# Reordering the first loads and the start-up steps of a packed-attention and gated-FFN kernel

## The chip, the cores and the metric

The kernel runs on one core of one Trainium2 chip. The metric is device time in microseconds (us) of one execution, the median of several runs; lower is better. Engines are named as the profile names them: PE (TensorE matmul), PEld (its weight loads), DVE (VectorE), ACT (ScalarE), POOL (GpSimd) and SP (SyncE, which here only issues DMAs; SPq in the rows).

## What is computed

For 8 batches and 8 heads, 32 packed queries `p` first attend to 576 keys and values, and the 576 queries `q` then attend to the 32 packed results. The heads are joined to a 512-wide row for each of 8 x 576 = 4608 tokens, and a gated feed-forward layer follows.

```python
def sm_attn(qq, kk, vv):
    s = scale * np.matmul(qq, kk.transpose(0, 1, 3, 2))
    s = s - np.max(s, axis=-1, keepdims=True)
    a = np.exp(s)
    a = a / (np.sum(a, axis=-1, keepdims=True) + 1e-09)
    return np.matmul(a, vv)
p_packed = sm_attn(p, k, v)                  # softmax 1: 32 x 576 per head
out = sm_attn(q, p_packed, p_packed)         # softmax 2: 576 x 32 per head
x = out.transpose(0, 2, 1, 3).reshape(B * S, H * D)
return (x @ w_a) * (x @ w_b) @ w_out         # 512 -> 1536 (twice) -> 512
```

## The kernel before

**The algebra.** The attention output is never formed. For each batch and slice of weight columns the kernel multiplies the packed results with the weights first (`g_tiles`, L357, 16 matmuls at L371, "G"), and then G with the softmax-2 weights (`mm1`, L394, matmuls at L389). The product of the two halves is h; `mm2_part` (L412) multiplies it with w_out. Large products run as three passes on a high and a low word (hi x hi, hi x lo, lo x hi). The high word is a cast on ACT, the low word a subtraction on DVE or POOL (`lo_part`, L90).

**Order of work.** `manual_schedule` (L570) keeps every engine, SP too, in the order in which the program emits its instructions. So the order is written by hand, as strings of short names that `emit` (L458) reads:

- `FIRST` (L499): the first loads on SP. `k0`, `k1` are heads 0 to 3 and 4 to 7 of batch 0's k for its first 512 tokens (512 KB each, `load_first`, L131), `k2` the last 64 tokens of all heads (128 KB); the same for q. `p0` is three DMAs of 32 KB (`load_p`), `v0` and `v1` are one of 512 KB and two of 32 KB each (`load_v`), `w1` is one raw weight piece of 512 KB (`load_w`).
- `START` (L500): what follows before the first `mm1`. `T0` turns p and `P0` the packed results (two PE transposes, one copy, L241 and L243). `k0`..`k4` and `q0`..`q4` turn the loaded k and q on PE (`turn_first`, L142): n = 0, 1 use part 0, n = 2, 3 part 1, n = 4 part 2; the copy out of PSUM is on DVE or ACT, as `TURN` (L503) says for each. `S0` starts softmax 1 of the even heads (e = 0); every `r0` is its next step (score matmuls L255; maximum and exponential; reciprocal; transposes L291; product with v L301); `r1` and `S1` step the odd heads (e = 1). `s0` and `s1` step softmax 2 of the two halves (`stage2`, L310): score matmuls L316; transpose and maximum on DVE (L321, L325); subtraction (L328); exponential on ACT (L330); sum and reciprocal on DVE, scaling (L334 to L337); transpose into `a2f` on DVE (L341) and high-word cast on ACT (L347); low word on DVE. `SUBS` (L504) says for each batch and half whether the subtraction and the scaling are on DVE ("1") or POOL ("0").
- `A`, `B`, `C`: the weights arrive as 36 raw pieces (24 of w_a and w_b, numbered 0 to 23, then 12 of w_out) and each goes through three conversions, in order of the pieces: A is the high word on ACT (L194), B the low word (L196) on ACT, DVE or POOL as the piece's digit in `WAYS` (L502) says ("0", "1", "2"; L202 for ACT, L199 for the other two), C joins them on DVE (L205) and frees the raw buffer, upon which SP loads a further piece. There are 12 raw buffers. `D` splits a finished w_out piece (cast on ACT, low word on POOL). G of a pair of slices needs four C more than the pair before.
- `W` (L557): nine matmuls on data already there, whose result nobody uses; they fill PE. `g` is the first G. `Lk`, `Lq`, `Lv`, `Lp` are loads for batch 1 and later.
- `PLAN_0` (L509): the same names for batch 0's 12 slices of `mm1` (24 slots, two for each slice: one between its two halves, one at its end) and the first of `mm2` after it; `PLAN` (L506) for batch 1. `k0` and `k1` of batch 1 are DVE transposes (L124), its `S0` stands in slot 11.

**Buffers that tie the engines together.** `mm1` takes two PSUM bank pairs "m" in turn. ACT empties one (`asb`, L401), DVE multiplies the other with it (L404), ACT casts the product (L408) and POOL makes its low word (`h_lo`, L91). `asb` has two buffers, so that slice n+2 needs the `h_lo` of slice n. G, the turned tiles and several transposes share two PSUM banks "x". At most eight DMAs of SP are under way: the ninth waits for the first to land, and so on.

After batch 1 the kernel goes over to another scheme (L685 on) for batches 2 to 7, which the change does not touch.

Of the kernel before, what the change touches and what calls it, by code (L numbers as in the profile page):

```python
# [19 lines left out]
def tile_packed_attn_gated_ffn(  # L20
# [21 lines left out]
    B, H, S, D = q.shape  # L42
# [50 lines left out]
    def bank():  # L93
        return ps_x.tile([P, 512], F32, name="x")

    def bank_pair(s=False):
        return ps_s.tile([P, 2, 512], F32, name="s") if s else ps_m.tile([P, 2, 512], F32, name="m")
# [44 lines left out]
    def turn_first(key, n):  # L142

        if (0, key) not in xTs:
            pool = scratch if key == "q" else ld
            xTs[0, key] = [pool.tile([P, R, HS], F32, name=f"xT{i}") for i in range(2)]
        copy = (nc.vector.tensor_copy, nc.scalar.copy)[int(TURN["kq".index(key) * 5 + n])]
        x = bank_pair()[:, 0, :] if n in (2, 3) else bank()
# [47 lines left out]
    def low_word(raw, way):  # L196
        low = raw[..., 0]
        if way:
            (nc.vector if way == 1 else nc.gpsimd).tensor_scalar(  # L199
                out=low, in0=low, scalar1=2.0 ** -29, scalar2=7.0, op0=ALU.mult, op1=ALU.min)  # L200
        else:
            nc.scalar.activation(out=low, in_=low, func=AF.Copy, scale=0.93 * 2.0 ** -29)  # L202
# [107 lines left out]
    def stage2(b, e):  # L310
# [15 lines left out]
        yield  # L326
        eng = nc.vector if b < 2 and SUBS[2 * b + e] == "1" else nc.gpsimd
        eng.tensor_tensor(out=s2, in0=s2, in1=mx.unsqueeze(2).broadcast_to([P, TU, J]), op=ALU.subtract)  # L328
# [125 lines left out]
    def drain(g):  # L454
        for _ in g:
            pass

    def emit(b, plan, tasks={}):  # L458

        for name in plan.split():  # L460
            if name in tasks:
                next(tasks[name], None)
                continue
            if name == "W":
                warm()
                continue
            if name in "ABCD":
                convert(name)
                continue
            what, e = name[:-1], int(name[-1])  # L470
            n = b + (e // 2 if b or what[0] == "L" else 0)
            if n >= B:
                continue
            if what == "S":
                if e == 0:
                    st[b] = [stage1(b, 0), stage1(b, 1), stage2(b, 0), stage2(b, 1)]
                next(st[b][e])
            elif what == "s":
                next(st[b][2 + e], None)
            elif what == "r":  # L480
                next(st[b][e], None)
            elif what == "T":
                turned(pT, p_nat.pop(n))
            elif what == "P":
                turned(ppT[:, b % 2:b % 2 + 2], pp.pop(b), b % 2)
            elif what in ("k", "q"):
                turn(what, n, e % 2) if b else turn_first(what, e)
            elif what == "Lk":
                load(k, "k", n, e % 2)
            elif what == "Lq":  # L490
                load(q, "q", n, e % 2)
            elif what == "Lv":
                load_v(n, e % 2)
            elif what == "Lp":
                load_p(n)

    st = {}

    FIRST = ("p0 k0 k2 k1 q0 v0 q1 v1 q2 w1 w1 w1 w1 w1 w1 w1 w1 w1 w1 w1")  # L499
    START = ("T0 k0 k4 k1 k3 k2 q0 S0 S1 r0 r1 q1 r1 r0 r0 r1 r0 q2 r1 q3 q4 P0 s0 B s1 W A s0 B A A s0 s0 B s1 C "  # L500
             "A s1 B s0 C s1 A s1 C B B Lp2 C A B A s0 s1 B C B B s0 B g A C A A s1 Lv2 Lk2 C C A A C B B Lk3 C s1")
    WAYS = ("000000022220202120012012011200010010")  # L502
    TURN = ("0001110101")  # L503
    SUBS = ("0100")  # L504

    PLAN = (" |  |  | S0 | r0 | r0 |  | r0 |  | r0 Lv1 ; S1 | r1 | r1 q0 Lk2 | r1 | r1 | q1 Lk3 Lv2 P0 |  ; s0 | s0 s0 | s0 T2 | "  # L506
            "s0 Lp4 | s0 s1 | s1 s1 | s1 | s1 | s1 | t0 t1 t2 t3 u0 | k2 |  | k3 Lq2")
    PLAN = dict(enumerate(PLAN.split("|")))
    PLAN_0 = ("A | C C | B A B A | B C C B C | A A | C | B | C B A T0 k0 Lp2 A | A A B B C Lq0 | C C k1 | A B A | "  # L509
# [3 lines left out]
    PLAN_0 = dict(enumerate(PLAN_0.split("|")))  # L513

    pieces = [(c, n) for c in range(NC) for n in range(4)] + [(NC, f) for f in range(NFT)]
# [12 lines left out]
    def convert(x):  # L528
# [14 lines left out]
        elif x == "B":  # L543
            low_word(raw, int(WAYS[pieces.index((c, n))]))
        else:
# [18 lines left out]
    def next_g(b):  # L564

        g_tiles(b, *(((0, 1), (2,)) if b else ((0, 1),)), s=True)
        yield

    ET = mybir.EngineType
    ep(tc.manual_schedule(engines={ET.PE, ET.DVE, ET.Activation, ET.Pool, ET.SP}))  # L570
    for name in FIRST.split():
        what, i = name[0], int(name[1])
# [8 lines left out]
    tasks = {"g": next_g(0)}  # L581
    emit(0, START, tasks)
    drain(tasks["g"])
# [53 lines left out]
    for b in range(NB):  # L637
        plan = dict(PLAN if b else PLAN_0)
        slot, tasks, late_steps = [0], {"g": next_g(b + 1)} if b == 0 else {}, [""]
# [316 lines left out]
```

## Time and profile before

| | |
|---|---|
| median of 3 runs | 715.3 us (714.02, 715.3, 716.52) |
| the profiled execution | 714.0 us, of which the span of its instructions is 712.2 us |
| START (to the first `mm1` matmul) | 34.7 us |
| batch 0 (`mm1`, `mm2`) up to the first `mm1` of batch 1 | 34.7 to 122.9 us |
| the untouched scheme of batches 2 to 7 | from about 172 us on |

A row of a timeline reads: start, duration, engine, line, operation, what it writes and reads, shapes, count, and in brackets the time for which the engine had been idle before and what released it. A row of a table by stages reads: the stretch, its length, then for each engine its busy time and its number of instructions, the granted TensorE clock, the mean busy share of the DMA engines and their rate in GB/s.

### The profile page before, as it was taken

To read this page: it belongs to the slowest core of one execution; us is meant where nothing else is said; L and a number is where in the kernel's file an instruction comes from. 1 tells how busy PE (TensorE), PEld (TensorE's weight loads), DVE (VectorE), ACT (ScalarE), POOL (GpSimd) and SP (SyncE) were. 2 spreads that over 40 slices of the span, in tenths; PEclk is the share of its full clock that TensorE was granted. 3 is DMA by queue.
4 is the path that set the end of the run, shared out by engine and by line. 5 is a ranking of instruction groups with operands and counts; after the bars stand their busy time and mean duration, and the time that the engine had idled before them with its cause. 6 is when DMAs were issued, how large, how long until landed. Compare 5 with 4: busy or idle time off the path is not lost.

```text
span 712.2 us, 14198 instructions
## 1 busy us (share of the span) xinstructions
PE 699.0 (98%) x5558; PEld 574.2 (81%) x5558; DVE 449.8 (63%) x819; ACT 363.2 (51%) x733; POOL 417.8 (59%) x322
## 2 busy tenths in 40 slices
PE   6899999999999999999999999999999999999998
PEld 4488877888778887887888788788888888888887
DVE  3888755367455669665875668765785657754342
ACT  3788753554344455644563456554554455544520
POOL 0496753337334687745874579566776578856520
PEclk9999999999999999999999999999999999999999
DMA  8999872767344735555453574457146323133002
GB/s 230 387 274 315 220 162 53 193 153 282 93 98 139 211 96 141 139 138 146 134 111 115 142 195 93 106 176 182 61 98 180 105 89 119 61 110 127 1 1 74
DMA packets 177059, 102.37 MB, mean 144 GB/s; under 512 B 141280, under 2 KB 159456, under 8 KB 171616
## 3 DMA queue, kind: packets, MB, share of 16 engines
q1 hardware_dynamic: 176992, 101.47, 50.3%
q8 instruction: 43, 0.70, 0.4%
q14 instruction: 24, 0.20, 0.1%
HBM read 85.72 MB, written 15.73 MB: 142 GB/s over the span
## 4 chain that ended last, share of the span: by engine, by line
PE 94%; DVE 2%; SPq 1%; DMA 1%; ACT 1%; issue 0%; DVEq 0%; ACTq 0%
PE x L724 37%; PE m L765 29%; PE m L389 9%; PE x L779 5%; PE m L415 5%; PE s L301 2%; PE s L316 1%; PE s L255 1%; PE x L371 1%; PE s L291 1%; SPq L116 1%; DMA kn<-in_k_dram 1%; DMA nat<-in_k_dram 0%; PE m L152 0%; PE x L152 0%
## 5 line engine op out<-in xcount | busy, mean ns | idle before, releaser
L724 PE MATMUL x<-wo,h_hi 128*128 128x512 f32 (+1 forms) x776 | 249.3, 391 | 0.0
L91 POOL TENSOR_TENSOR h_lo<-asb,h_hi 128x576 fp32r<-128x576 f32 x96 | 140.3, 1462 | 83.3 <-ACT h_hi L810 44.6
L724 PEld LDWEIGHTS x<-wo,h_hi 128*128 128x128 f32 x776 | 140.8, 188 | 22.2 <-ACT gs L785 1.0
L724 PE MATMUL x<-wo,h_lo 128*128 128x512 f32 (+1 forms) x388 | 152.1, 392 | 0.0
L91 POOL TENSOR_TENSOR G_lo<-gs,G_hi 128x640 fp32r<-128x640 f32 x72 | 113.0, 1575 | 30.6 <-ACT G_hi L800 30.3
L724 PEld LDWEIGHTS x<-wo,h_lo 128*128 128x128 f32 x388 | 72.9, 188 | 11.8
L91 POOL TENSOR_TENSOR A_lo<-gs,A_hi 128x256 fp32r<-128x256 f32 x36 | 27.2, 754 | 89.7 <-ACT A_hi L788 89.7
L847 DVE TENSOR_TENSOR d<-m,d 128x576 f32<-128x576 f32 (+1 forms) x73 | 54.0, 740 | 34.6 <-ACT d L843 33.8
L860 DVE TENSOR_TENSOR asb<-m,d 128x288 f32<-128x288 f32 x72 | 32.4, 451 | 66.4 <-ACT c L856 64.8
L856 ACT COPY c<-m 128x288 f32<-128x288 f32 x72 | 28.8, 399 | 78.6 <-PE m L765 78.6
L734 DVE TENSOR_TENSOR part<-x,part 128x512 f32<-128x512 f32 (+1 forms) x65 | 44.1, 678 | 38.8 <-PE x L724 38.8
L765 PE MATMUL m<-tx_hi,G_hi 128*128 128x288 f32 x216 | 63.8, 296 | 0.0
L765 PE MATMUL m<-tx_hi,G_lo 128*128 128x288 f32 x216 | 63.7, 295 | 0.0
L785 ACT COPY gs<-x 128x512 f32<-128x512 f32 x36 | 21.1, 587 | 82.8 <-PE x L779 81.2
L765 PE MATMUL m<-tx_lo,G_hi 128*128 128x288 f32 x216 | 63.3, 293 | 0.0
L800 ACT CAST G_hi<-gs 128x640 fp32r<-128x640 f32 x72 | 52.2, 730 | 15.1 <-POOL gs L794 14.5
L843 ACT COPY d<-m 128x576 f32<-128x576 f32 (+1 forms) x73 | 46.6, 639 | 20.2 <-PE m L765 18.6
L810 ACT CAST h_hi<-asb 128x576 fp32r<-128x576 f32 x72 | 49.0, 680 | 11.5 <-DVE asb L874 11.5
L765 PEld LDWEIGHTS m<-a_hi,G_hi 128*128 128x128 f32 x144 | 27.0, 187 | 31.6 <-issue 17.4
L794 POOL TENSOR_TENSOR gs<-gs 128x512 f32<-128x512 f32 x36 | 46.7, 1296 | 2.6 <-DVE gs L791 2.5
L765 PE MATMUL m<-a_hi,G_hi 128*128 128x288 f32 x144 | 47.0, 326 | 0.0
L389 PE MATMUL m<-a_hi,ghi 128*128 128x288 f32 x192 | 43.2, 307 | 1.5 <-ACT ghi L377 1.5
(171 smaller groups left out, 1548.7 us busy)
## 6 DMA issues: line engine op xcount, KB each, us to landing
wr<-w_kept SPq DMA_DIRECT2D x36, 1024.0 KB
nat<-in_k_dram SPq DMA_DIRECT2D x56, 144.0 KB
nat<-in_q_dram SPq DMA_DIRECT2D x56, 144.0 KB
vt<-in_v_dram SPq DMA_DIRECT2D x28, 256.0 KB
out_dram<-part SPq DMA_DIRECT2D x27, 256.0 KB
raw<-in_moe_w_a_dram SPq DMA_DIRECT2D x12, 512.0 KB
raw<-in_moe_w_b_dram SPq DMA_DIRECT2D x12, 512.0 KB
raw<-in_moe_w_out_dram SPq DMA_DIRECT2D x12, 512.0 KB
```

Source lines behind the costliest of these rows:

```text
L91: return eng.tensor_tensor(out=dst, in0=src, in1=hi.bitcast(F32), op=ALU.subtract)
L389: nc.tensor.matmul(out=ps[:, half, 0:HS], lhsT=gt[:, kt, ft % 4, cols], rhs=at[:, kt, HS * half:HS * half + HS], start=(n == 0 and kt == 0 ...
L415: nc.tensor.matmul(out=o[:, cols], lhsT=ht[:, c0:c0 + P], rhs=wt[:, cols], start=(ft == 0 and n == 0), stop=(ft == NFT - 1 and n == 2))
L724: nc.tensor.matmul(out=o[:, cols], lhsT=ht[:, c0:c0 + P], rhs=wt[:, cols], start=(ft == fts[0] and n == 0), stop=end)
L734: nc.vector.tensor_tensor(out=parts[i][:, cols], in0=o[:, cols], in1=parts[i][:, cols], op=ALU.add)
L765: nc.tensor.matmul(out=bank[:, n % 2, 0:HS], lhsT=g, rhs=t, start=(first and i == 0), stop=(i == 2), skip_group_check=True)
L779: nc.tensor.matmul(out=gps[e][J * r:J * r + J, :], lhsT=ppT[rows, 2 * (b % 2), r, :], rhs=w[rows, r, :], start=True, stop=True)
L794: nc.gpsimd.tensor_tensor(out=gs[:, 2:4].rearrange("p a u f -> p a (u f)"), in0=gs[:, 0:2].rearrange("p a u f -> p a (u f)"), in1=s2.unsqu ...
L800: nc.scalar.copy(out=G_hi[:, n % 3], in_=gs[:, 1:6, n % 2])
L810: nc.scalar.copy(out=view(h_hi[ft]), in_=src)
L843: nc.scalar.copy(out=d[:, both], in_=X[:, both, 0:HS])
L847: nc.vector.tensor_tensor(out=d[:, both], in0=V[:, both, 0:HS], in1=d[:, both], op=ALU.add)
```

## The change

Only the strings change; `PLAN` is only joined into one literal. In `FIRST`, k2 and k0 go ahead of p0, q1 and q0 ahead of v0, and q2 goes behind three weight pieces. In `START`, `T0` moves behind k1, the turns of q and the steps of softmax 1 are interleaved otherwise, and the conversions stand at other places. `WAYS` gives 16 low words to POOL instead of 10, 9 to DVE instead of 7, 11 to ACT instead of 19; among the first 13, which are converted in START, POOL had 7, 8, 9, 10, 12 and now has 1, 5, 7, 9, 10, 11, 12. `TURN` swaps the engines of several copies. `SUBS` puts the subtraction and scaling of batch 0's second half on POOL; both were on DVE. In START `Lk2 Lk3` (k of batch 1) now stand ahead of `Lv2`. `PLAN_0` is written anew; the turns, softmax steps and loads of batch 1 keep nearly the same slots, and the conversions are spread otherwise.

```diff
-    FIRST = ("p0 k0 k2 k1 q0 v0 q1 v1 q2 w1 w1 w1 w1 w1 w1 w1 w1 w1 w1 w1")
-    START = ("T0 k0 k4 k1 k3 k2 q0 S0 S1 r0 r1 q1 r1 r0 r0 r1 r0 q2 r1 q3 q4 P0 s0 B s1 W A s0 B A A s0 s0 B s1 C "
-             "A s1 B s0 C s1 A s1 C B B Lp2 C A B A s0 s1 B C B B s0 B g A C A A s1 Lv2 Lk2 C C A A C B B Lk3 C s1")
-    WAYS = ("000000022220202120012012011200010010")
-    TURN = ("0001110101")
-    SUBS = ("0100")
+    FIRST = ("k2 k0 p0 k1 q1 q0 v0 v1 w1 w1 w1 q2 w1 w1 w1 w1 w1 w1 w1 w1")
+    START = ("k0 k4 k1 T0 k2 k3 S0 r0 q2 r1 q3 q0 S1 r0 r1 r0 r1 q1 r0 B r1 A A B q4 P0 s0 s0 s1 C s0 A s1 s1 W s0 B Lp2 C s0 B B s1 C A B B A A s1 A C A s0 B C A B B B s1 s0 s1 C B g A C A C A s1 C Lk2 Lk3 C Lv2 B")
+    WAYS = ("020002020222202022121112211201120120")
+    TURN = ("0110110010")
+    SUBS = ("0000")
...
-    PLAN_0 = ("A | C C | B A B A | B C C B C | A A | C | B | C B A T0 k0 Lp2 A | A A B B C Lq0 | C C k1 | A B A | "
-              "S0 B | B A r0 | C C C | B A Lq1 |  | C C B r0 r0 D A A | S1 C D | B C B B A D | r1 C | A A D | r0 T2 "
-              "|  | q0 B r1 C B D r1 C |  | A | D B C Lv1 A r1 | A B D Lk2 B C B q1 D Lk3 A A P0 | C s0 s0 D C Lp4 "
-              "A B | s1 s0 | Lv2 | D | s0 s1 s0 | k2 s0 s1 C k3 | s1 |  | Lq2 D s0 s1 s1 Lq3 s1")
+    PLAN_0 = ("A C | | A A | C | B C B B | A C B C C B B A | | A A T0 Lq0 B k0 A C | B Lp2 C A | B k1 C B | A C | C A S0 B | B r0 C A | Lq1 B C | A | C | r0 C r0 D B A | S1 A C B D | C A B D B | r1 C | r1 D | A r0 A C | T2 | B q0 D A r1 | | C B Lv1 A B D | C A r1 | A B Lk2 C B q1 D C P0 | D D s0 B Lk3 C | s0 Lv2 B s1 | s0 A Lq2 D s0 s1 | | | s0 k2 D s0 s1 s0 s1 C Lp4 s1 A k3 | | | s1 Lq3 s1")
```

More of the change, by code (lines that the diff above doesn't have):

```diff
@@ L497, in tile_packed_attn_gated_ffn @@
     st = {}
-    FIRST = ("p0 k0 k2 k1 q0 v0 q1 v1 q2 w1 w1 w1 w1 w1 w1 w1 w1 w1 w1 w1")
-    START = ("T0 k0 k4 k1 k3 k2 q0 S0 S1 r0 r1 q1 r1 r0 r0 r1 r0 q2 r1 q3 q4 P0 s0 B s1 W A s0 B A A s0 s0 B s1 C "
-             "A s1 B s0 C s1 A s1 C B B Lp2 C A B A s0 s1 B C B B s0 B g A C A A s1 Lv2 Lk2 C C A A C B B Lk3 C s1")
-    WAYS = ("000000022220202120012012011200010010")
-    TURN = ("0001110101")
-    SUBS = ("0100")
-    PLAN = (" |  |  | S0 | r0 | r0 |  | r0 |  | r0 Lv1 ; S1 | r1 | r1 q0 Lk2 | r1 | r1 | q1 Lk3 Lv2 P0 |  ; s0 | s0 s0 | s0 T2 | "
-            "s0 Lp4 | s0 s1 | s1 s1 | s1 | s1 | s1 | t0 t1 t2 t3 u0 | k2 |  | k3 Lq2")
+    FIRST = ("k2 k0 p0 k1 q1 q0 v0 v1 w1 w1 w1 q2 w1 w1 w1 w1 w1 w1 w1 w1")
[3 more added lines that the diff above has]
+    SUBS = ("0000")
+    PLAN = (" |  |  | S0 | r0 | r0 |  | r0 |  | r0 Lv1 ; S1 | r1 | r1 q0 Lk2 | r1 | r1 | q1 Lk3 Lv2 P0 |  ; s0 | s0 s0 | s0 T2 | s0 Lp4 | s0 s1 | s1 s1 | s1 | s1 | s1 | t0 t1 t2 t3 u0 | k2 |  | k3 Lq2")
     PLAN = dict(enumerate(PLAN.split("|")))
-    PLAN_0 = ("A | C C | B A B A | B C C B C | A A | C | B | C B A T0 k0 Lp2 A | A A B B C Lq0 | C C k1 | A B A | "
[3 rows of a table removed]
+    PLAN_0 = ("A C | | A A | C | B C B B | A C B C C B A | | A A T0 Lq0 B k0 A C | B Lp2 C A | B k1 C B | A C | C A S0 B | B r0 C A | Lq1 B C | A | C | r0 C r0 D B A | S1 A C B D | C A B D B | r1 C | r1 D | A r0 A C | T2 | B q0 D A r1 | | C B Lv1 A B D | C A r1 | A B Lk2 C B q1 D C P0 | D D s0 B Lk3 C | s0 Lv2 B s1 | s0 A Lq2 D s0 s1 | | | s0 k2 D s0 s1 s0 s1 C Lp4 s1 A k3 | | | s1 Lq3 s1")
     PLAN_0 = dict(enumerate(PLAN_0.split("|")))
```

## The prediction

> **What bounds the kernel now.** I read the page first, then a table by stages.
>
> ```profile
> span 712.2 us, 14198 instructions
> PE 699.0 (98%) x5558; PEld 574.2 (81%) x5558; DVE 449.8 (63%) x819; ACT 363.2 (51%) x733; POOL 417.8 (59%) x322
> ```
> ```profile
> 5.00:10.00 5.00, 3.00 (x17) 2.52 (x17) 1.12 (x2) 0.43 (x2) 0.00 (x0) 1.00 1.11 311
> 15.00:20.00 5.00, 4.46 (x100) 3.27 (x100) 2.23 (x11) 3.25 (x9) 0.00 (x0) 1.00 1.11 307
> 0.00:37.27 37.27, 27.61 (x270) 16.84 (x270) 21.90 (x43) 20.70 (x40) 10.67 (x12) 1.00 0.96 310
> 37.27:172.00 134.73, 134.49 (x1249) 113.57 (x1250) 88.94 (x142) 81.53 (x149) 73.39 (x49) 1.00 0.77 206
> 700.00:712.20 12.20, 9.17 (x52) 7.89 (x50) 2.92 (x5) 0.00 (x0) 0.00 (x0) 0.98 0.34 108
> ```
> PE is idle for 13.2 us in all: 9.66 before 37.27, 3.03 in the tail that the change leaves alone, and 0.24 in the rest of the stretch that `PLAN_0` governs and the start of the next. So the change can win only before 37.27, but can lose anywhere up to 172. Next, PE's timeline in the start.
>
> ```profile
> 7.08 1.12 PE L152 MATMUL x<-ident,kn 128*128 128x128 f32 x4 [2.00 <-DMA kn<-in_k_dram]
> ...
> 10.03 1.92 PE L152 MATMUL m<-ident,kn 128*128 128x128 f32 x8
> ...
> 17.89 0.66 PE L152 MATMUL m<-ident,qn 128*128 128x128 f32 x4
> ...
> 21.55 0.72 PE L316 MATMUL s<-xT,ppT 64*32 64x288 f32 x16 [0.61 <-DVE ppT L243]
> ...
> 23.46 7.99 PE L562 MATMUL m<-kn,ident 128*128 128x512 f32 x18
> 31.63 1.57 PE L371 MATMUL x<-w_ab,ppT 64*32 64x512 f32 x16 [0.17 <-DVE w_ab L205]
> 34.68 0.54 PE L389 MATMUL m<-a_hi,ghi 128*128 128x288 f32 x2 [1.48 <-ACT ghi L377]
> ...
> 37.27 0.54 PE L389 MATMUL m<-a_lo,ghi 128*128 128x288 f32 x2 [0.26 <-DVE a_lo L91]
> ```
> 7.99 us of PE's busy time are the filler `W`. The time is therefore set by when softmax 2 can start (21.55) and by how long DVE, ACT and POOL need from there to feed `mm1` without a break (37.27).
>
> **The start, up to s0.** SP's timeline and the chain of waits:
>
> ```profile
> 0.74 1.96 SPq L182 DMA_DIRECT2D p_nat<-in_p_dram  x3
> 2.74 0.48 SPq L135 DMA_DIRECT2D kn<-in_k_dram  x1
> ...
> 38.01 1.78 SPq L170 DMA_DIRECT2D vt<-in_v_dram  x2
> ```
> ```profile
> 2.74 4.30 DMA kn<-in_k_dram
> ...
> 39.99 6.69 PE m L389 x48
> ...
> 55.20 2.89 DMA nat<-in_k_dram
> ```
> With k2 alone ahead of it, k0 is issued at 0.74 plus one first issue, about 1.5, not 2.74. At 4.30 us to landing that is 5.8, not 7.04; the three small transfers of p no longer go ahead, which may spare up to 0.9. I take 5.5 (4.9 to 5.8). From k0's landing to the copy that ends `P0` took 13.9 us (7.04 to 20.98, below). Three things are added. `T0`, formerly done while PE waited for k0, now stands behind k1: 0.9. The copy of q4 moves from ACT to DVE, ahead of that of `P0`: 0.43 (row below). And turns of q now stand between the two halves of softmax 1, so that ACT makes two copies of q ahead of the second exponential: walked step by step, 0.3 net. So 5.5 + 15.5 = 21.0, and s0 at 21.5: no gain, although k lands 1.5 us earlier.
>
> The eight turns of k2 and k3 took 1.92 us at 10.03 and would take 1.3 at the later pace of 0.66 for four; the granted clock stands at 1.00 in both stretches. I count half of that difference as won, since PE now starts 1.5 us earlier and has no break. The Trainium skill ("TensorE: Matmul & The Clock Gate", Part 1) lets PE run fast after some 3.4 us of steady work; the trace still shows slow turns three us after 7.08. By the rule the sum would be 0.3 lower.
>
> q4 needs q2, which now goes behind three weight pieces: 5088 KB in all with k, p, q and v, 5.2 MB. At the 0.307 to 0.311 MB/us of the rows, from a start near 3.5, it lands at about 20.2. PE has done the turn's predecessors at 19.9, so q2 costs 0 to 0.3. The end of a transfer can trail the mean rate: k0's 512 KB at that rate are 1.7 us, not 4.30. So up to 1.2 more is the upper end.
>
> **From s0 to a steady `mm1`.**
>
> ```profile
> 20.61 0.43 ACT L159 COPY xT<-x 128x128 f32<-128x128 f32 x2 [1.44 <-PE x L157]
> ```
> ```profile
> 20.98 0.42 DVE L243 COPY ppT<-x 128x256 f32<-128x256 f32 x1 [0.29 <-PE x L241]
> 22.36 0.78 DVE L321 STREAM_TRANSPOSE s<-s 128x576 f32<-128x576 f32 x1 [0.96 <-PE s L316]
> ...
> 25.33 0.71 DVE L205 SCALAR_TENSOR_TENSOR w_ab<-raw 128x512 uint32<-128x512 uint32 x1
> ...
> 29.81 1.08 DVE L337 TENSOR_TENSOR s<-s,sum 128x576 f32<-128x576 f32 x1
> ...
> 32.01 1.42 DVE L341 STREAM_TRANSPOSE a2f<-s 128x576 f32<-128x576 f32 x2
> ...
> 34.66 1.29 DVE L91 TENSOR_TENSOR glo<-x,ghi 128x512 fp32r<-128x512 f32 x2
> ...
> 36.46 0.76 DVE L91 TENSOR_TENSOR a_lo<-a2f,a_hi 128x576 fp32r<-128x576 f32 x1
> ```
> ```profile
> 24.02 1.16 POOL L328 TENSOR_TENSOR s<-s,mx 128x576 f32<-128x576 f32 x1 [22.71 <-DVE mx L325]
> 28.03 1.41 POOL L337 TENSOR_TENSOR s<-s,sum 128x576 f32<-128x576 f32 x1 [2.86 <-DVE sum L336]
> 29.63 12.54 POOL L199 TENSOR_SCALAR raw<-raw 128x512 uint32<-128x512 uint32 x5 [0.19 <-DMA raw<-in_moe_w_b_dram]
> 42.24 1.43 POOL L91 TENSOR_TENSOR h_lo<-asb,h_hi 128x576 fp32r<-128x576 f32 x1
> ```
> ```profile
> L199 POOL TENSOR_SCALAR raw<-raw x10: 2000/2344/2971, 29.6 to 76.5; 128x512 uint32<-128x512 uint32 x10
> ```
> Now the walk for the second half, s1. Its transpose and maximum stand behind the first join C (0.71) and end at 26.05, where the old order had them at 25.4. The subtraction is on POOL (1.16): 27.3. The exponential on ACT stands behind two low words: 28.0. Sum and reciprocal on DVE, behind another C: 30.0. The scaling goes to POOL, too, and there B5 is emitted ahead of it. POOL scales the first half until 29.5, then B5 takes 2.0 to 2.5 (I take 2.3): 31.9. Then the scaling, 1.3: 33.3. Before, DVE had it at 30.9. So the transpose of s1 ends at 34.05, not 33.43. Behind it DVE has, in emitted order, two low words of a2f, one C and only then the low words of G (0.7, 0.7, 0.65, 0.65): the first at 36.75. The old order had G's low words ahead, at 34.66, and the second a2f word last. PE starts `mm1` near 34.9 but after four matmuls needs that word; where the old order had done 14 matmuls by 37.27, ten are left. At 6.69/48 = 0.139 each they end at 38.1. **Cost 0.85**, less 0.05 for s0. `W` and the first G change nothing: the filler runs until about 31.4 either way, and the fourth C is done by then.
>
> **POOL's backlog, 38 to 66 us.** The steps that follow on ACT:
>
> ```profile
> L377 ACT CAST ghi<-x 128x512 fp32r<-128x512 f32 x9 | 4.8, 583 | 0.0
> L408 ACT CAST h_hi<-asb 128x576 fp32r<-128x576 f32 x7 | 4.7, 671 | 2.7 <-DVE asb L404 2.7
> L401 ACT COPY asb<-m 128x576 f32<-128x576 f32 x7 | 4.5, 637 | 0.4 <-PE m L389 0.4
> ```
> ```profile
> 59.72 0.71 PE L255 MATMUL s<-xT,pT 64*32 64x288 f32 x20 [0.20 <-DVE xT L124]
> ```
> From 33.3 POOL has B7, B9, B10, B11, B12, two `h_lo`, B14. With B at 2.0 to 2.5, taken as 2.3 and then 2.1 once DVE joins less: B10 ends at 40.4, `h_lo` of slice 0 at 46.3 (43.7 before), B14 at 50.0. Who waits?
> - C10 (slot 0) waits on DVE for B10, with the product of slice 0 queued behind it: product at 41.8, cast 0.67, two casts of G 1.17, copy 0.64 on ACT: bank pair free at 44.25, PE wants it at 43.95. **0.3.**
> - C14 (slot 5) waits for B14; behind it stand C15, B18 and the low words of the third G until 52.4, which hold the "x" bank that `T0` of batch 1 needs; PE wants it at 51.8. **0.6.**
> - In slots 8 to 10 DVE has B20 to B22, k1, C and two low words of G ahead of the product of slice 5: 63.1, wanted at 62.65. **0.45.**
> - A gain: SP issues k of batch 1 ahead of v, so at least 1.78 earlier, and its last part, which landed at 58.09 (55.20 + 2.89), no longer holds up `S0` in the row of 59.72. The first four of its 24 matmuls were issued 0.88 ahead of the rest, of which they need 0.3. **-0.6.**
>
> At no B above 2.0 the first two items vanish; at 2.5 throughout they are 0.8 and 2.2.
>
> After 66 I count nothing. PE needs G and the w_out pieces far apart there, DVE, ACT and POOL are busy for 89, 82 and 73 of 135 us, and six more low words on POOL are 14 us in its gaps. Were the gaps not where the words fall, each could cost up to 2.3.
>
> **Sum.** 0.8 + 0.3 + 0.6 + 0.45 - 0.6 = 1.55: the profiled execution's 714.0 becomes 715.5. The median of the runs shown is 715.3, so I forecast 716.8. That is no change that a measurement of this kernel can tell, which takes about 0.3%, 2.15 us.
>
> **Rivals.**
> - *POOL's backlog in full* (slower). If B runs at the 12.54/5 = 2.5 of its busiest row, as it did with DVE joining beside it, the two stalls grow by 0.5 and 1.6: 718.9. It decides from 2.3 on. For it: seven of the first 13 low words are on POOL now and h_lo stands behind them. Against: DVE has idle time beside B5. 0.20.
> - *q2 late* (slower). All that follows shifts by up to 1.3: 718.1. For it: the three pieces ahead. Against: the mean rate holds it at 20.2. 0.12.
> - *An exclusive port* (slower). In the first 12.6 us of POOL's low words, DVE ran these joins beside them:
>
> ```profile
> 29.60:42.20 12.60, 7.07 (x10) 1.00 1.04 362
> ```
> Were they to add their full time to five words of 2.0, these would take 17.1, not 12.54. If now some nine two-input steps of 0.7 added theirs, B14 would end at 54.5 and the sum grow by 4.5: 721. The Trainium skill ("SBUF - State Buffer", SBUF: two separate sides) says that a GpSimd instruction and a DVE one with two SBUF inputs shut each other out for a whole instruction; by that rule this rival holds, by the trace a third of it does. 0.03.
> - *The early k comes through* (faster). k0 at 4.9 shifts all by -0.6, B at 2.0 brings the scaling 0.3 forward and takes the two stalls away: 716.8 - 0.6 - 0.3 - 0.9 = 715.0, and without the third 714.5. For it: 1.2 us fewer of issues ahead of k. Against: q2 and the longer chain behind k0. 0.23.
>
> **The numbers.** The forecast has 0.42. Slower by over 0.3%: the first three rivals, 0.35. Faster by over 0.3%: the last rival reaches that only with the 1.3 by which runs of one kernel differ (714.02 to 715.3), 0.14 with what I may have overlooked; the rest, 0.51, is no change. The range goes from 714.5 less 1.3, 713.2, to 718.9 with part of q2's delay, 719.6.
>
> **What would show it.** Right: k0's first turn near 5.6; s0 within 0.5 of 21.55; L337 twice on POOL, the second past 31.5 with an L199 between; the first `glo` behind both `a_lo`, near 36; PE idle near 44 and 52 for `asb` and `glo`; no idle time at batch 1's `S0`. Wrong: s0 at 20.5 or before, or past 22.5; `mm1` steady by 37; PE unbroken from there to 66; or new idle time of PE past 66.

## The result, and the profile after

| | before | after |
|---|---|---|
| median | 715.8 us (714.02 to 716.52) | 725.0 us (724.24 to 725.49) |
| profiled execution | 714.0, span 712.2 | 725.38, span 723.5 |

The ratio after to before is 1.0132 (95% interval 1.0110 to 1.0154): 9.3 us slower by the medians. The forecast was 716.8 with a range to 719.6. First the page of the kernel after:

```profile
span 723.5 us, 14200 instructions
...
PE 703.5 (97%) x5558; PEld 575.7 (80%) x5558; DVE 454.6 (63%) x820; ACT 358.4 (50%) x724; POOL 433.6 (60%) x330
```

Now its table by stages, cut where the steady `mm1` starts (40.37 instead of 37.27) and 11.2 us behind the place of before (172.00):

```profile
0.00:40.37 40.37, 28.13 (x261) 15.96 (x261) 20.40 (x41) 20.61 (x39) 14.43 (x14) 0.91 0.96 309
40.37:183.20 142.83, 138.33 (x1259) 116.05 (x1260) 95.17 (x145) 76.58 (x141) 85.11 (x55) 0.99 0.70 188
```

PE is idle for 12.24 us ahead of 40.37 (9.66 before) and for 4.50 in the second stretch (0.24 before). Over the whole execution it is also busy for 4.5 us more (703.5 against 699.0) with the same 5558 matmuls: some of them ran slower. PE's timeline in the start shows where:

```profile
22.39 0.77 PE L157 MATMUL x<-ident,qn 32*128 32x32 f32 x8 [2.28 <-DMA qn<-in_q_dram]
...
24.29 1.21 PE L316 MATMUL s<-xT,ppT 64*32 64x288 f32 x16 [0.52 <-DVE ppT L243]
...
26.40 9.55 PE L557 MATMUL m<-kn,ident 128*128 128x512 f32 x18
...
38.40 0.54 PE L389 MATMUL m<-a_hi,ghi 128*128 128x288 f32 x2 [1.43 <-ACT ghi L377]
...
40.37 0.85 PE L389 MATMUL m<-a_hi,glo 128*128 128x288 f32 x2 [1.17 <-DVE glo L91]
41.01 0.68 PE L389 MATMUL m<-a_hi,ghi 128*128 128x288 f32 x2
```

Three rows answer to rows of before. PE waits 2.28 us for q2, and s0 is at 24.29 instead of 21.55. The filler `W` takes 9.55 us instead of 7.99. The first `mm1` pairs from 41.01 on take 0.68 instead of 0.43. The granted clock of the TensorE (the third column from the right) says why:

```profile
20.00:25.00 5.00, 2.21 (x34) 1.41 (x34) 1.20 (x4) 1.28 (x2) 1.98 (x1) 0.77 1.06 357
25.00:30.00 5.00, 5.00 (x33) 1.92 (x14) 4.32 (x7) 1.17 (x3) 2.19 (x2) 0.54 1.05 384
...
40.00:45.00 5.00, 4.63 (x36) 4.14 (x36) 4.99 (x8) 1.69 (x3) 4.76 (x4) 0.68 0.83 258
```

It was 1.00 in these stretches before. Now POOL's and DVE's timelines in the start:

```profile
32.85 2.02 POOL L199 TENSOR_SCALAR raw<-raw 128x512 uint32<-128x512 uint32 x1
34.95 1.39 POOL L337 TENSOR_TENSOR s<-s,sum 128x576 f32<-128x576 f32 x1
36.42 10.57 POOL L199 TENSOR_SCALAR raw<-raw 128x512 uint32<-128x512 uint32 x5
```
```profile
36.37 0.78 DVE L341 STREAM_TRANSPOSE a2f<-s 128x576 f32<-128x576 f32 x1 [1.05 <-POOL s L337]
37.08 1.57 DVE L91 TENSOR_TENSOR a_lo<-a2f,a_hi 128x576 fp32r<-128x576 f32 x2
38.56 1.15 DVE L205 SCALAR_TENSOR_TENSOR w_ab<-raw 128x512 uint32<-128x512 uint32 x1
39.64 1.28 DVE L91 TENSOR_TENSOR glo<-x,ghi 128x512 fp32r<-128x512 f32 x2
```

As forecast, the second scaling (L337) stands behind a low word on POOL, and the first `glo` behind both `a_lo` and a join. Last, PE's waits behind 50, and the rows of DVE and of POOL that belong to the first two:

```profile
57.67 0.44 PE L241 MATMUL x<-ident,p_nat 128*128 128x128 f32 x2 [1.08 <-DVE glo L91]
...
64.80 0.53 PE L389 MATMUL m<-a_hi,ghi 128*128 128x288 f32 x2 [0.68 <-DVE asb L404]
...
66.59 0.72 PE L255 MATMUL s<-xT,pT 64*32 64x288 f32 x24
...
70.37 0.53 PE L389 MATMUL m<-a_hi,ghi 128*128 128x288 f32 x2 [0.74 <-DVE asb L404]
...
92.38 0.53 PE L389 MATMUL m<-a_hi,ghi 128*128 128x288 f32 x2 [0.62 <-DVE asb L404]
...
96.39 0.73 PE L415 MATMUL m<-wo,h_hi 128*128 128x512 f32 x2 [0.68 <-DVE asb L404]
```
```profile
54.48 2.54 DVE L205 SCALAR_TENSOR_TENSOR w_ab<-raw 128x512 uint32<-128x512 uint32 x2 [0.84 <-POOL raw L199]
56.94 1.28 DVE L91 TENSOR_TENSOR glo<-x,ghi 128x512 fp32r<-128x512 f32 x2
...
61.09 2.98 DVE L205 SCALAR_TENSOR_TENSOR w_ab<-raw 128x512 uint32<-128x512 uint32 x2
64.00 0.74 DVE L404 TENSOR_TENSOR asb<-m,asb 128x576 f32<-128x576 f32 x1
```
```profile
54.52 1.94 POOL L91 TENSOR_TENSOR h_lo<-asb,h_hi 128x576 fp32r<-128x576 f32 x1
...
61.04 1.43 POOL L91 TENSOR_TENSOR h_lo<-asb,h_hi 128x576 fp32r<-128x576 f32 x1
```

From 54.48 two joins take 2.54 us together, from 61.09 two take 2.98, where a pair in the flow takes 1.3. In each pair one join alone takes 1.93 (55.09 to 57.02 and 61.09 to 63.02), and beside each POOL runs an `h_lo`, until 56.46 and 62.47: both joins end 0.55 us behind it. The `glo` that frees `T0`'s bank and the product that PE awaits at 64.80 stand behind these joins.

**Where the 11.3 us of the two spans lie.** Three marks divide them: s0, the second G (38.80 before, 44.49 after) and the end. Up to s0 2.7 were lost, from s0 to the second G 2.95 (17.25 became 20.20), behind it 5.6 (673.4 became 679.0). I use the last two lengths for all runs below, since the start of s0 itself varies: in four runs with the same loads and the same steps up to it, e10, e11, e13 and e14, it was at 22.6 or 22.7 (22.0 in e5), where the profiled execution of before had 21.55. Part of the 2.7 is thus chance, and it fits that the medians differ by 9.3 and not by 11.3.

### The profile page after: what moved, and what is told of

The parts are those of the page before. It is cut to its first block, busy times and chain, and to the rows that moved or that the text cites. A ratio compares the mean times of both kernels' runs of the same rounds, so it can differ in the third digit from the quotient of the medians.

```text
span 723.5 us, 14200 instructions
## 1 busy us (share of the span) xinstructions
PE 703.5 (97%) x5558; PEld 575.7 (80%) x5558; DVE 454.6 (63%) x820; ACT 358.4 (50%) x724; POOL 433.6 (60%) x330
## 4 chain that ended last, share of the span: by engine, by line
PE 86%; DMA 4%; POOL 3%; DVE 3%; issue 1%; SPq 1%; ACT 1%; DVEq 0%; ACTq 0%; POOLq 0%
PE x L719 37%; PE m L760 29%; PE m L389 6%; PE x L774 5%; PE m L415 4%; PE s L301 1%; DMA raw<-in_moe_w_b_dram 1%; PE s L316 1%; DMA raw<-in_moe_w_a_dram 1%; POOL raw L199 1%; PE s L255 1%; DMA qn<-in_q_dram 1%; POOL h_lo L91 1%; DVE w_ab L205 1%; POOL wo L91 1%
## 5 line engine op out<-in xcount | busy, mean ns | idle before, releaser
L91 POOL TENSOR_TENSOR h_lo<-asb,h_hi 128x576 fp32r<-128x576 f32 x96 | 141.1, 1471 | 86.0 <-ACT h_hi L805 44.4
L91 POOL TENSOR_TENSOR G_lo<-gs,G_hi 128x640 fp32r<-128x640 f32 x72 | 113.1, 1576 | 30.6 <-ACT G_hi L795 30.3
L91 POOL TENSOR_TENSOR A_lo<-gs,A_hi 128x256 fp32r<-128x256 f32 x36 | 27.2, 755 | 89.6 <-ACT A_hi L783 89.6
L838 ACT COPY d<-m 128x576 f32<-128x576 f32 (+1 forms) x73 | 46.7, 640 | 20.1 <-PE m L760 18.5
L805 ACT CAST h_hi<-asb 128x576 fp32r<-128x576 f32 x72 | 49.0, 680 | 11.3 <-DVE asb L869 11.3
L389 PE MATMUL m<-a_hi,ghi 128*128 128x288 f32 x192 | 44.0, 311 | 3.5 <-DVE asb L404 2.0
```

Source lines behind the costliest of these rows:

```text
L91: return eng.tensor_tensor(out=dst, in0=src, in1=hi.bitcast(F32), op=ALU.subtract)
L389: nc.tensor.matmul(out=ps[:, half, 0:HS], lhsT=gt[:, kt, ft % 4, cols], rhs=at[:, kt, HS * half:HS * half + HS], start=(n == 0 and kt == 0 ...
L805: nc.scalar.copy(out=view(h_hi[ft]), in_=src)
L838: nc.scalar.copy(out=d[:, both], in_=X[:, both, 0:HS])
```

## The experiments

"Before" is the old kernel's median beside the run named. The theories were formed in turn; their numbers in the expectations are those of that time.

### The loads

e1 is the changed kernel with q2 ahead of all weight pieces, e2 the changed kernel with the whole old `FIRST`, e3 the old kernel with the changed `FIRST`.

```diff
-    FIRST = ("k2 k0 p0 k1 q1 q0 v0 v1 w1 w1 w1 q2 w1 w1 ...
+    FIRST = ("k2 k0 p0 k1 q1 q0 v0 v1 q2 w1 w1 w1 w1 w1 ...      # e1
```

> The changed kernel, with q2 loaded ahead of the weight pieces again and nothing else altered. Changed kernel: 725.0 us, softmax 2 (s0) at 24.3, filler from 26.4 to 35.9, first mm1 matmul at 38.4. Theory A (q2's place costs a wait of 2.3 us and, through the cold clock, 0.5 more, and everything behind moves with it): s0 at 21.7, first mm1 near 35.4, 721.8. Theory B (the filler, stretched by the cold clock, gates the first G as well): 720.3. Theory C (the steps on DVE and POOL after 40 us set the end whatever happens before): above 723.5.

> The changed kernel with the whole old order of the first loads (p0 k0 k2 k1 q0 v0 q1 v1 q2 w...). k0 then lands at 7.04 instead of 5.1, q2 at 17.6 instead of 22.2. If the long chain behind k0 (15 us from k0 to the turn of q4) sets s0, s0 comes at about 23.5 and the time is 724; if the place of q2 is all that the load order cost, s0 comes at 21.6 and the time is 721.8.

> The kernel before with only the new order of the first loads. Theory A: q4 has to wait for q2 as in the changed kernel (landing at 22.2 instead of 17.6), s0 at about 24, a cold clock, and +2.7 to +3.2 us: 718.5 to 719. If the load order costs nothing by itself in the old order of steps: 715.8.

Measured, beside 715.1 for before: e1 722.84 (ratio 1.0115, 1.0095 to 1.0136), e2 725.41 (1.0152, 1.0132 to 1.0171), e3 715.88 (1.0014, 1.0002 to 1.0026). By e1, q2's late landing costs the changed kernel some 2.2 us if the two medians are compared, 1.5 if each is taken against the before beside it. This size is not settled: in e2 q2 is early, too, and s0 came at 22.5 instead of 24.3, but nothing was gained. In the old order of steps the new loads cost 0.8. Most of the loss lies in the steps.

### The clock

e4 is the changed kernel with three filler matmuls ahead of the turn of q4; e9 is e1 with three between the first G and the first `mm1`.

```diff
-  ... A A B q4 P0 ...            # e4, from the changed START
+  ... A A B V q4 P0 ...
-  ... C B g A C A ...            # e9, from e1
+  ... C B g V A C A ...          # V: warm(3)
```

> The changed kernel with three more filler matmuls just ahead of the turn of q4, so that PE is busy while it waits for q2; q2 lands as late as before. Granted clock should stay near 1.00 in 20 to 30 us (0.77 and 0.54 in the changed kernel). Theory A: s0's own matmuls are quick again, 0.5 us won, 724.5. Theory B: the filler ends 1.5 us earlier and the first G with it, 723.5. If the clock is of no weight: 725.0.

> The run e1 (changed kernel, q2 ahead of all weight pieces) with three more filler matmuls, whose result nobody uses, between the first G and the first mm1. In e1 PE is idle there for 3.2 us and runs the mm1 matmuls behind it at a pitch of 0.24 us instead of 0.134. Theory (the idle time cools PE's clock and the cooling is what makes some 2 of e1's lost us): the pitch is 0.134 from the start, the second G 1.5 to 2 us after the place it had in e1 less the idle, that is near 40 instead of 41.8, and the time is 720.5 to 721.5. Rival (mm1 waits at that place for its low words anyway, or the lost time is lost again in PLAN_0's stalls): within 0.5 of e1's 722.8.

e4: 726.05 (1.0162, 1.0146 to 1.0178), nothing gained: `W` then took 7.99 us again, but it had not been what ended last. PE waited for `ghi` instead, 3.26 us where it had been 1.43. e9: 720.54 (1.0087, 1.0073 to 1.0100) against e1's 722.84. PE's timeline of e1 and of e9, and the granted clock from 35 to 40 of both:

```profile
35.46 0.53 PE L389 MATMUL m<-a_hi,ghi 128*128 128x288 f32 x2 [3.23 <-ACT ghi L377]
...
37.43 0.85 PE L389 MATMUL m<-a_hi,glo 128*128 128x288 f32 x2 [1.18 <-DVE glo L91]
38.08 0.68 PE L389 MATMUL m<-a_hi,ghi 128*128 128x288 f32 x2
```
```profile
35.00:40.00 5.00, 3.37 (x14) 3.13 (x15) 5.00 (x8) 2.57 (x5) 4.76 (x4) 0.74 1.04 365
```
```profile
34.71 0.53 PE L389 MATMUL m<-a_hi,ghi 128*128 128x288 f32 x2 [0.47 <-ACT ghi L377]
...
36.69 0.53 PE L389 MATMUL m<-a_hi,glo 128*128 128x288 f32 x2 [1.17 <-DVE glo L91]
37.06 0.43 PE L389 MATMUL m<-a_hi,ghi 128*128 128x288 f32 x2
```
```profile
35.00:40.00 5.00, 3.83 (x32) 3.15 (x39) 5.00 (x7) 2.97 (x6) 4.84 (x3) 1.00 1.02 320
```

The fillers of e9 cut the idle time ahead of the first `mm1` from 3.23 to 0.47 us. The first `mm1` still comes 13.6 us behind s0 in both, and both wait 1.2 us for `glo`. But e1's pairs then take 0.68, those of e9 0.43, and from s0 to the second G there are 19.9 us in e1 and 18.5 in e9. The cooled clock is thus shown to cost 1.5 us at this place; the two medians differ by 2.3, or by 1.8 if each is taken against the before beside it.

### The parts alone, and taken back

e5 is the old kernel with the changed `PLAN_0` alone, e6 the changed kernel with the old one; e7 the old kernel with the changed `WAYS` alone; e8 the changed kernel with the old `SUBS` ("0100"), e10 the old one with the changed `SUBS` ("0000"). Each is an exchange of that one string.

> The kernel before with the changed PLAN_0 alone (loads, START, WAYS, TURN and SUBS are the old ones). In the changed kernel 5.6 of the 11.3 us of the span were lost behind the second G, in stalls of PE at batch 1's T0 and, for the product of slices, near 64, 69, 91, 95 and 140. Theory 1 (the stalls come from the backlog that START leaves and from the added low words on POOL and DVE; the spread of the conversions over the slots is harmless): within 1.5 us of the kernel before, 715 to 717. Rival 2 (the new spread itself puts C and low words ahead of products that PE waits for): the same stalls show here, 718.5 to 721.

> The changed kernel with the old PLAN_0 alone. Theory 1: the losses up to the second G stay (about 5.7 us) and those behind it stay in great part, since START, WAYS and the backlog are unchanged: 722 to 726. Rival 2 (the spread itself): the stalls near 64, 69, 91 and 95 go, the losses up to the second G stay: 719.5 to 721. In both cases s0 near 24.3 and the second G near 44.5.

> The kernel before with the changed WAYS alone: 16 low words on POOL instead of 10, 9 on DVE instead of 7, 11 on ACT instead of 19, all at the old places. If the added words on POOL and DVE are what PE waits for, whatever the order (rival 3), stalls on the product or on w_out show behind 60 and the time is 718 to 722; of the first seven words two (pieces 1 and 5) then stand on POOL ahead of softmax 2's steps, too, which could delay the steady mm1 by up to 2. If the order decides (theory 1), the gaps of POOL hold the words: 715 to 717.

> The changed kernel with SUBS as before: the subtraction and the scaling of batch 0's second half back on DVE, everything else changed. Theory 1 holds that the scaling, behind a low word on POOL until near 34.9, delays s1 and with it the low words of G by 1 to 3 us: the second G comes by 41.5 to 43 instead of 44.5, the time is 722 to 724. Rival 4 (the joins and low words that the new START puts ahead on DVE and ACT are the cost, not the place of two steps): within 0.7 of the changed kernel's time, 724.5 to 725.5.

> The kernel before with SUBS 0000 alone: subtraction and scaling of the second half on POOL, where no low word stands ahead of them in the old START. The chain from s0 to the first mm1 is then 1.86 us shorter on DVE (0.78 and 1.08 in the row of before) and a2f of the second half bound by POOL. Theory (the move to POOL is not the harm, the words that the new START puts ahead of it are): same or up to 1.5 us faster, 713.5 to 715.3. Rival (POOL's slower steps and its late start on the low words cost): 715.8 to 717.

| run | time | before | ratio (95%) | s0 to second G | behind it |
|---|---|---|---|---|---|
| before, profiled | | | | 17.25 | 673.4 |
| after | 725.04 | 715.77 | 1.0132 (1.0110 to 1.0154) | 20.2 | 679.0 |
| e5, `PLAN_0` alone | 719.64 | 714.82 | 1.0075 (1.0060 to 1.0090) | 17.1 | 677.6 |
| e6, old `PLAN_0` | 720.82 | 714.82 | 1.0093 (1.0073 to 1.0112) | 21.0 | 673.1 |
| e7, `WAYS` alone | 716.88 | 714.82 | 1.0035 (1.0022 to 1.0049) | 18.6 | 673.8 |
| e8, old `SUBS` | 725.18 | 714.82 | 1.0153 (1.0138 to 1.0168) | 20.0 | 678.8 |
| e10, `SUBS` alone | 715.08 | 714.61 | 1.0002 (0.9993 to 1.0011) | 16.7 | 674.4 |

My theory 1, that `PLAN_0` only shows a backlog which `START` and `WAYS` build, fell twice: alone it costs 4.8 us, and with the old one the changed kernel loses nothing behind the second G. The waits of PE from 39 to 140, e6 first and e5 below (place, releaser, total, times, longest):

```profile
PE m L389 <- ACT ghi L377: 2.2, 1, 2.2
PE m L389 <- DVE glo L91: 0.6, 1, 0.6
```
```profile
PE x L241 <- DVE glo L91: 0.9, 1, 0.9
PE m L415 <- DVE asb L404: 0.7, 1, 0.7
PE m L389 <- DVE asb L404: 0.6, 2, 0.4
PE m L371 <- ACT asb L401: 0.4, 1, 0.4
PE m L389 <- ACT asb L401: 0.4, 1, 0.4
```

e6 keeps the start's two waits alone; e5 has those at `T0` (L241), for the product (`asb` by DVE), ahead of `mm1` (L389) and of `mm2` (L415), and two for ACT's copy of a bank pair (`asb` by ACT). The one of these ahead of `mm1`, at 44.42, fits the wait of 0.3 that the prediction gave to C10. The 0.74 that after has at 70.37 is in neither list. The place of the second half's subtraction and scaling is worth nothing (e8, e10). `WAYS` alone costs 2.1 us by the medians; 1.4 of it lies between s0 and the second G, where PE's wait for `ghi` grew from 1.48 to 2.03 and the clock fell behind it. PE's timeline of e7, then two rows of its table by stages and one of before's, each 3.41 us long:

```profile
36.16 0.54 PE L389 MATMUL m<-a_hi,ghi 128*128 128x288 f32 x2 [2.03 <-ACT ghi L377]
```
```profile
33.46:36.87 3.41, 1.38 (x16) 0.56 (x4) 2.87 (x6) 3.13 (x6) 3.33 (x2) 1.00 1.05 384
36.87:40.29 3.42, 3.42 (x15) 3.40 (x15) 3.42 (x6) 2.62 (x5) 3.26 (x3) 0.50 0.84 256
```
```profile
32.36:35.77 3.41, 1.94 (x18) 0.93 (x7) 3.41 (x6) 2.96 (x6) 3.33 (x2) 1.00 1.06 387
```

In the stretch that holds the idle time PE is busy for 1.38 us in e7, and the clock of the next is 0.50; in before it is busy for 1.94, and the clock stays at 1.00.

### PLAN_0 in two halves

e11 is e5 with two joins of slot 5 moved to slot 8. (The changed slot 5 is `A C B C C B A`, as here; the diff of the change shows one `B` more.) e13 is the old kernel with the changed slots 0 to 14 alone, e14 with the changed slots from 15 on.

```diff
-  | A C B C C B A | | A A T0 Lq0 B k0 A C | B Lp2 C A |       # e11, from e5
+  | A C B B A | | A A T0 Lq0 B k0 A C | B Lp2 C C C A |
```

> The run e5 (old kernel with the changed PLAN_0) with the two joins of slot 5 moved to slot 8, behind T0 and k0 of batch 1. Theory (joins that wait on DVE for low words just emitted hold up the low words of the third G and with them the x bank of T0): the stall of 1.1 us at T0 near 52 goes, and the time falls to 718 to 719. Rival (the sum of DVE's work in those slots is the cost, wherever the joins stand): the stall moves to a later slot, 719.2 to 720.2.

> The kernel before with the changed slots 0 to 14 of PLAN_0 and the old ones from 15 on (at the seam both plans stand at 25 high words, 25 low words and 23 joins). The whole changed PLAN_0 cost 4.8 (e5). By PE's stalls in e5 (0.3 and 0.5 near 42 and 44, 1.1 at T0 near 52, 0.3 near 64) these slots hold 2.2 of it: 716 to 717.5. Rival (the stalls of the second half, for the product and w_out near 85 and 89 and behind 133, are the consequence of a backlog built up here): 718.5 to 719.7.

> The kernel before with the old slots 0 to 14 of PLAN_0 and the changed ones from 15 on. By the stalls in e5 (0.5 near 85, 0.9 near 89, 0.8 near 134) these hold 2.2 to 2.6 of the 4.8: 716.8 to 718, with the stalls near 85 and 89 in its trace. Rival (they follow from the first half's backlog): 714.6 to 715.6, without these stalls.

e11: 719.57 (1.0073, 1.0059 to 1.0087). The stall at `T0` fell from 1.1 to 0.3 us between matmul starts and nothing was gained: the fourth G came 17.3 us behind the second instead of 17.7, the fifth another 9.8 later instead of 9.1. The place of two joins is not it. e13: 717.44 (1.0040, 1.0027 to 1.0054), e14: 716.9 (1.0029, 1.0015 to 1.0043), beside 714.47. Their 3.0 and 2.4 add up to 5.4, against 4.8 for the whole: each half has its own loss, and e14's trace holds the waits for the product at L389 (0.5) and L415 (0.7) with the old first half ahead of them.

What the halves have in common are long joins beside two-input steps of POOL, as in the profile after. Here are e14's at its first wait for the product, DVE and then POOL, and last the join of before at the same place:

```profile
81.64 1.89 DVE L205 SCALAR_TENSOR_TENSOR wo_f<-raw 128x512 uint32<-128x512 uint32 x1 [1.75 <-POOL wo L91]
...
83.71 0.76 DVE L404 TENSOR_TENSOR asb<-m,asb 128x576 f32<-128x576 f32 x1
```
```profile
81.56 1.42 POOL L91 TENSOR_TENSOR h_lo<-asb,h_hi 128x576 fp32r<-128x576 f32 x1
```
```profile
80.02 1.90 DVE L205 SCALAR_TENSOR_TENSOR wo_f<-raw 128x512 uint32<-128x512 uint32 x1 [0.69 <-POOL wo L91]
```

The join waits 1.75 us for a low word of w_out, starts beside the `h_lo` that POOL takes next, lasts 1.89, and the product stands behind it; near 86 it is the same with 1.61. In before the join at this place is as long and the product stands behind it, too (at 81.84), but the join had waited only 0.69 for its word, and PE did not wait. Summed over the joins past 40 that run beside L91 on POOL, the time above 0.68 is 2.2 us in before, 2.5 in e6, 5.3 in e5, 4.0 in e11, 5.0 in e13, 2.2 in e14 and 5.6 in after. (The sums in the expectation of e18 are up to 1.3 higher, and its 1.97 should be 1.93: they took some records of waits on DVE for joins.) The sum is thus high wherever the changed first half is in, though e11 has less of it than e5 and was no faster. In the second half it is not the sum that changed: the word of w_out comes some 1 us later (counted from the fifth G), and with it the long join and the product. e18 tests the collision: it is e5 with these POOL steps reading one input, so that the true low words of h (batches 0 and 1) and of w_out are left out.

```diff
-        lo_part(h_lo[ft][:, c0:c0 + S], flat, hh, nc.gpsimd)      # subtract(flat, hh)
+        nc.gpsimd.tensor_scalar(out=h_lo[ft][:, c0:c0 + S], in0=hh, 2.0 ** -13, 7.0, mult, min)
```

> The run e5 (old kernel, changed PLAN_0), with the low words of h and of w_out on POOL made by a step that reads one input (the high word times a constant) instead of two; it leaves out the true low words, so that the output lacks their part. Why: in e5's trace the joins on DVE (two inputs) that run beside these two-input steps of POOL take up to 1.97 us instead of 0.68, and end some 0.55 behind the POOL step. Summed over the joins this excess is 6.6 us in e5 and 6.9 in the changed kernel, 2.2 in the kernel before, 5.0 and 3.5 in e13 and e14. Theory (a two-input step of POOL and a join shut each other out, and the changed PLAN_0 puts more joins beside them): no join beside these steps takes over 0.8, PE's waits near T0 and for the product go from 2.5 to under 1, and the length behind the second G falls from 677.6 to 673.5 to 675, the time to 715.3 to 717. Rival (the long joins wait for their words): they stay near 1.9, and the time stays at 719 to 720.5.

e18: 717.37 beside 714.86 (1.0040, 1.0023 to 1.0058), against 1.0075 for e5. DVE's and POOL's timelines at the place that answers to 54.48 in after:

```profile
51.25 1.76 DVE L209 SCALAR_TENSOR_TENSOR w_ab<-raw 128x512 uint32<-128x512 uint32 x2 [0.84 <-POOL raw L203]
```
```profile
51.30 2.64 POOL L94 TENSOR_SCALAR h_lo<-h_hi 128x576 fp32r<-128x576 f32 x1
```

The pair of joins takes 1.76 us beside a POOL step of 2.64. No join beside these steps takes over 1.15 (0.8 had been expected), the excess is 2.6 us, and PE's waits for the product near 85 and 89 are gone: the join there takes 0.69. By the medians 2.5 of the 4.8 us remain, and the intervals of the two ratios just miss each other, so the collision of two-input steps is a part of the cause, about half. The profiled execution does not show this gain: it was one of e18's longer ones (719.12, of 715.80 to 721.82), and from the second G on it took 677.6 us, as e5 did, where 673.5 to 675 had been expected. What it saved at the product it lost near 64, where PE waited 1.68 for `asb` behind a late weight piece and the clock then fell to 0.50 from 65.11 to 68.53: from the fourth G to the fifth there are 11.9 us, 9.1 in e5. The collision is not all, either: the joins near 51 still wait 0.84 for a word of POOL, PE still waits 0.8 at `T0`, and the one-input step took 2.13 us, not 1.43, so that e18 gives POOL more work. How the other half of `PLAN_0`'s loss divides is not shown.

### START, and what is left

e12 is the changed kernel with the old `PLAN_0`, e1's loads, and softmax 2 and G ahead of the conversions between `W` and `mm1`; e16 is e12 with three filler matmuls behind G.

```diff
-  W s0 B Lp2 C s0 B B s1 C A B B A A s1 A C A s0 B C A B B B s1 s0 s1 C B g A C A C A s1 C
+  W s0 s1 B Lp2 C s0 s1 B B C A B B A A A C A s0 s1 B C A s0 g B B B s1 C B A C A C A s1 C
```

> The changed kernel with the old PLAN_0, q2 ahead of the weight pieces, and START rearranged only between W and the first mm1: the steps of softmax 2 and the first G stand ahead of the low words, joins and casts between them (same tokens, other order); WAYS, TURN and SUBS stay changed. From e6 and e1 the same kernel without the rearrangement would take about 718.6. Theory (what START lost lies in the order between W and mm1: exponential and scaling of the second half behind ACT's and POOL's low words, G's low words behind joins): first mm1 near 34.5, second G by 39.5, 714.5 to 716.5. Rival (the moved low words, or the longer way to s0, are the cost): 717.8 to 719.5.

> The run e12 (old PLAN_0, q2 early, START rearranged behind W) with three filler matmuls between the first G and the first mm1, where e12's PE was idle for 2.8 us and then ran at a granted clock of 0.52. Theory (what is left of START's loss is the cooled clock): 715.2 to 716.3. Rival (the longer chain to the first mm1 costs by itself): 717 to 718.

e12: 718.02 (1.0049, 1.0034 to 1.0064), e16: 717.61 (1.0045, 1.0030 to 1.0060). Both theories failed. In e12 the first `mm1` came at 36.3, not 34.5: PE idled 2.81 us for `ghi` and then ran cold. In e16 it ran warm and had the second G 2.8 us earlier, at 39.5, but behind it 676.5 us instead of 674.3: at 60.76 PE had waited 1.39 us for the product. PE came earlier there, DVE and POOL did not. What remains of e16's 3.1 us over before is not assigned to a single step.

### The early k

e15 is the old kernel with k2 and k0 ahead of p0 and `T0` behind k1, all else old; e17 is e15 with `Lv2` moved behind `Lk3`.

```diff
-    FIRST = ("p0 k0 k2 k1 q0 ...      START = ("T0 k0 k4 k1 k3 k2 ...
+    FIRST = ("k2 k0 p0 k1 q0 ...      START = ("k0 k4 k1 T0 k3 k2 ...
```

> The kernel before, with k2 and k0 loaded ahead of p0 and T0 behind k1, all else old (q2 stays ahead of the weight pieces). If s0 hangs on k0's landing, it comes some 0.5 to 1.2 earlier and the time is 713.6 to 714.6; if on the last of q and v, or if PE waits for softmax 2's chain in a way that takes it back, 714.6 to 715.5.

> The run e15 with both loads of batch 1's k issued ahead of that of its v (Lv2 moved behind Lk3), as the changed START has it. In e15 PE's score matmuls of batch 1 wait near 58 to 59 for the transpose of k, which waits 1.0 us on DVE for the load. If the stall goes with the earlier load: 0.3 to 1.0 faster than e15, 712.5 to 713.2. If DVE's transpose is then late for another reason, or v becomes late: 713.4 or more.

e15: 713.46 beside 714.47 (ratio 0.9989, 0.9980 to 0.9998): s0 at 20.6, about 1 us won, the only version faster than before, by a little over 0.1% (the prediction took 0.3% as the least that tells). e17: 714.15 beside 714.33 (0.9999, 0.9990 to 1.0008). PE's score matmuls of batch 1 ran unbroken, as they do in after, and nothing was gained; what took it back is not shown, but DVE and ACT now waited for a weight piece loaded later (2.17 us on DVE), and PE then 0.65 at 64.23 for ACT's copy. e15's timeline of PE, then e17's of PE and of DVE:

```profile
59.11 0.71 PE L255 MATMUL s<-xT,pT 64*32 64x288 f32 x20 [0.39 <-DVE xT L124]
```
```profile
58.44 0.72 PE L255 MATMUL s<-xT,pT 64*32 64x288 f32 x24
```
```profile
62.38 0.43 DVE L199 TENSOR_SCALAR raw<-raw 128x512 uint32<-128x512 uint32 x1 [2.17 <-DMA raw<-in_moe_w_b_dram]
```

## Why the prediction was wrong

Most of the places named were right; the terms were mis-sized, and two mechanisms were missing from the sum.

- **"q2 costs 0 to 0.3"**: q2 landed at 22.3 and cost 2.28 us of PE's time, 1.5 to 2.2 in the end (e1). The step that failed is the mean rate as a landing time. SP issued q2 only at 14.59 (10.93 before), and it landed 7.7 us later. I had written that the end of a transfer can trail the mean rate, allowed 1.2 for that, and took the lower value.
- **The clock, a missing term.** Idle time of PE was priced at its own length. It also slows the matmuls behind it: 1.5 us in e1 against e9, and about half of what `WAYS` costs alone (in e7 pairs started 0.48 apart instead of 0.27, and from the first `mm1` to the second G there were 5.09 us instead of 4.12). "`W` and the first G change nothing" was wrong in this way, too (9.55), though e4 shows that `W` was covered.
- **0.8 for the first `glo`**: the order was as walked (scaling behind a low word, `glo` behind both `a_lo`), and from s0 to the second G the loss was 2.95. The term counted the chain without the slow clock: in e9, where the clock stayed at 1.00, the loss is 1.2.
- **0.6 at `T0`**: 1.08 measured; the joins wait 0.84 for POOL's word, as named, and then one of them takes 1.93, which was not. **0.45 at slice 5**: 0.74 at 70.37. **0.3 at C10** did not show in after, though a wait that fits it did in e5 (0.36 at 44.42); 0.68 at 64.80 for the product of slice 4 did, which I had not seen.
- **-0.6 for k of batch 1**: the stall went, but e17 suggests that this by itself is worth nothing measurable.
- **The slow turns at 10.03.** I read a granted clock of 1.00 there. The trace has no record of the clock before 11.88 (12.50 in after), and 1.00 is what the table prints where it has none. The time counted as half won did not come (1.97 us for the eight turns in after), and the first 24 score matmuls behind them took 1.82 us, those at 13.39 took 0.72. PE's earlier start was thus spent in part on slow matmuls.
- **"After 66 I count nothing."** The largest failed step. By e14 the slots from 15 on cost 2.4 us alone. I took shares of busy time for slack (89, 82 and 73 of 135 us), where what counts is which step stands ahead of the product when PE wants its banks.
- **The exclusive port, given 0.03.** I judged it by POOL's one-input words (L199), which the joins slow little, and applied that to all of POOL's steps. Beside the two-input `h_lo` a join took 1.93 us instead of 0.68, and `h_lo` 1.94 instead of 1.43. The rule weighed there, from the Trainium skill ("SBUF - State Buffer", SBUF: two separate sides), thus holds for these pairs by the rows of after, and e18 bears it out in part; beside L199 a join there took at most 1.15.

Of the other rivals, q2's came true beyond its price, POOL's backlog in the place but not by the mechanism: its words took 10.57/5 = 2.1 us, not 2.5. The early k won its 1 us only where the rest was left alone (e15).

## What to carry to other kernels

Price an idle stretch of PE by its length and by the matmuls behind it that will run slower, and look up how long the idle stretches of the old trace were that did no harm. Take a transfer's landing from the slowest comparable transfer in the trace, not from the mean rate. When a hand-written order is replaced as a whole, take each engine's queue slot by slot to the end of the new text, since low shares of busy time do not protect the one step that PE waits for; and look which two-input steps of DVE come to stand beside those of POOL.

## What the runs showed of the hardware

- **A short idle time cools PE's clock.** Idle times of 1.47 to 1.48 us ahead of the first `mm1` (before, e3, e10, e11) left the granted clock at 1.00; one of 2.03 (e7) was followed by 0.50, one of 2.81 (e12) by 0.52, and one of 1.68 in e18 by 0.50. The matmuls then started 0.24 us apart instead of 0.134. The Trainium skill ("TensorE: Matmul & The Clock Gate", Part 1) has the clock halve after an idle window of some 3.4 us: the half is what the rows show (0.50), the length that sufficed here is shorter.
- **The busy share of a stretch of 3.41 us goes with the clock of the next.** In these 20 traces the clock changes only on a grid of 3.41 us, and ahead of the tail it stayed low for 3.41 or 6.83. There, all nine stretches of the grid at 1.00 in which PE was busy for 1.6 us or less were followed by 0.50, as in e7 (1.38); none with 1.94 or more was, as in before (1.94); of the four between, two were (e18's 1.73 and e6's 1.90) and two were not. So the place of an idle time on this grid counts as well as its length.
- **Two-input steps of POOL and of DVE hold each other up.** Joins took up to 1.93 us beside L91 on POOL (0.68 alone), but at most 1.15 beside the one-input steps of e18. Five one-input words of POOL with six joins beside them took 10.57 us, 2.11 each; the one at 32.85, with two joins beside it, took 2.02.
- **The same code reaches s0 at different times**: 21.55 to 22.7 in the profiled executions with the old loads and steps.
